# Numerators of eight token tiles per product, all value tiles by way of DRAM, and a query stage in a written-out order

## The chip, the cores and the metric

One Trainium2 chip, one of its cores. A time is the device time of one launch in microseconds (us). The engines are named as in the profile: PE multiplies matrices (PEld is its weight load), DVE works on vectors, ACT evaluates activations and copies out of PSUM, POOL is the fourth engine with arithmetic of its own, SP issues the DMAs. Each engine works through its queue in order; semaphores carry the waits between them. The matmul results lie in PSUM, eight banks of 128 partitions by 512 float32, everything else in SBUF or in DRAM.

## The reference, cut to what matters

```python
# B, S, D, H = 1, 2048, 448, 16 ; Dh = 28
def _A_ref(x, wqkv, w_phi, wo):                      # linear attention
    q, k, v = split_heads(x @ wqkv)
    pq, pk  = einsum("bhsd,hdf->bhsf", q, w_phi), einsum("bhsd,hdf->bhsf", k, w_phi)
    phi_q   = concat([softmax(pq), softmax(-pq)], -1)   # 56 features a head
    phi_k   = concat([softmax(pk), softmax(-pk)], -1)
    kv, z   = einsum("bhsf,bhsd->bhfd", phi_k, v), phi_k.sum("s")
    num     = einsum("bhqf,bhfd->bhqd", phi_q, kv)
    den     = einsum("bhqf,bhf->bhq", phi_q, z)[..., None] + 1e-6
    return (num / den) merged over heads @ wo
def _B_ref(x, wqkv, wo):                             # softmax attention
    q, k, v = split_heads(x @ wqkv)
    return softmax(q @ k.T * Dh ** -0.5) @ v merged over heads @ wo
g = sigmoid((x * gate_w).sum(-1, keepdims=True))
out = g * _A_ref(A_x, ...) + (1 - g) * _B_ref(A_x, ...)
```

Both branches take `A_x`. All inputs and the output are float32.

## The kernel before, in words

The program has four stages. Numbers of tokens: 2048 make 16 tiles of 128.

1. **Projection** (0 to some 62 us). x is split into a high part `XH` and a low part `XL` (float32r each), both kept in SBUF for all 2048 tokens; the keys and queries of branch B are multiplied in blocks of 512 tokens (`proj_qk`) and written to DRAM (`qkd`).
2. **Key stage** (62 to 180 us). For each of the 16 token tiles the folded key weights give the key features of branch A (`tok_major`, `features1`, the exponential in `take_exps`, `features2`), `value_a` the values, and `kv_add` sums their product in PSUM.
3. **Query stage** (180 to 350 us), a loop over q from 0 to 26 with conditions on q. Its steps:
   - *query tile* (16 times): eleven matmuls `pq` against `wqA_s`; `features1` copies it out on ACT (L465), takes the largest and smallest value of a head on DVE (L467, L468), and subtracts them on POOL (L471, L473) into one of four buffers `feat`; then the exponential on ACT (L476); `features2` sums and inverts on DVE (L483, L484) and multiplies on POOL (L485); `turn` transposes on DVE (L548) into `fT`. `fT` holds four tiles and has one buffer, so tile 4 can be turned only when the numerators of tiles 0 to 3 are multiplied.
   - *value tile* (`value_b`): eleven matmuls `pvb` against `wvB_s`, copied out on ACT (L765). Ten of the 16 tiles (`EARLY`) go into a buffer `ve` and by DMA to DRAM (`v_d`), to be fetched later by `load_early`; the buffers `vb` in which they end lie in memory that is free only later. Tile 7 is written straight into `vb` late in this stage, tiles 11 to 15 after it.
   - *numerators* (`numer(n, half)`): for four token tiles, 32-row by 32-column weights from `KV` against 128 columns of `fT`, 64 calls a half. A call of float32 stands in the trace as two matmuls. The result `pn` takes both `mx` buffers of PSUM.
   - *normalisation* of the eight results of 128x1024 (four n, two i): `normalize1` copies to `oU` on ACT (L416) and fetches the denominators by DMA (L421), `normalize2` inverts them on DVE (L427, L428) and spreads them through DRAM by DMA (L432, L437), `normalize3` multiplies on DVE (L443), `normalize4` splits into `oT` on ACT, DVE and POOL (L451, L452).
   - *output of branch A* (`out_a(n, a)`, 16 times): twelve matmuls `poa` against `woA_s`, scaled on ACT into `ga` (L602, two buffers) and written to DRAM by DMA (L603).
   - *maximum units* (`mx_unit`): four matmuls of 28 rows by 512 columns, a Relu of 128x1024 on ACT (L305) and two reductions on DVE (L307), for the upper bound that the softmax of branch B subtracts. Of the 56 units two are called in the first two rounds of this stage and 20 are spread by `tick`, which counts matmuls and calls a unit at each count in `pace["at"]`; the first twelve of these fall into the last rounds of the query loop (Relu tile `rl_s`), the other eight lie between the matmuls of the value tiles 11 to 15 (Relu tile `rl`).
   - at q = 21 the first query and key stacks of branch B are fetched from DRAM into `qk0` (`load_q(0)`, `load_nm(0)`, `load_k(0, 0)`).
   After the loop the pool `ta` and the weights `wp` are closed. In the memory that comes free lie the second half of `vb`, four further key stacks `kst`, one query stack `qst`; POOL clears the stacks (L781) before the DMAs fill them (L786). The value tiles 11 to 15 are multiplied in this time.
4. **Attention** (350 us to the end). For each group of four heads, block of 512 queries and tile of 128 keys: scores `st` (L1030), exponential on ACT (L1033), products with `vb` (L1129), and between them the rest of the maxima (`pm`, L339) and the output `pob`.

The order on PE, DVE, ACT and POOL is that in which the program is written (`manual_schedule`); the order of the DMAs on SP is the scheduler's. A tile that takes the place of another waits until the other has been read for the last time. PSUM in the query stage has two buffers of one bank (`s`, for `pq`, `pvb`, `poa`), two of two banks (`mx`) and one of two banks (`md`).

Of the kernel before, what the change touches and what calls it, by code (L numbers as in the profile page):

```python
# [8 lines left out]
F32 = mybir.dt.float32  # L9
# [31 lines left out]
def gated_mix_kernel(ctx, tc, xT, wqkB, wvB, wvA, wkAT, wqAT, phi, woA, woB,  # L41
# [39 lines left out]
    EARLY = (0, 1, 2, 3, 4, 5, 6, 8, 9, 10)  # L81
# [18 lines left out]
    XH = front.tile([P, 4, S], F32R, name="XH")  # L100
    XL = front.tile([P, 3, S], F32R, name="XL")
# [19 lines left out]
    def x3(t):  # L121

        for b in range(4):
            yield b, XH[:, b, t], 0
            yield b, XH[:, b, t], 1
            if b < 3:
                yield b, XL[:, b, t], 0

# [247 lines left out]
    def split_x(t, raws):  # L376
        tt = slice(t * 512, (t + 1) * 512)
        for b, raw in zip((0, 2), raws):
            nc.scalar.copy(XH[:, b:b + 2, tt], raw)

            def low(b=b, raw=raw):
                if b == 0:
                    nc.vector.tensor_sub(XL[:, 0:2, tt], raw, f32(XH[:, 0:2, tt]))
                else:
                    (nc.gpsimd if t > 1 else nc.vector).tensor_sub(
                        XL[:, 2, tt], raw[:, 0, :], f32(XH[:, 2, tt]))
                    nc.vector.tensor_sub(XH[64:, 3, tt], raw[64:, 1, :], f32(XH[64:, 3, tt]))

            lows.append(low)
# [22 lines left out]
    def normalize1(pool, pn, nm, n):  # L412

        oU = pool.tile([P, n, 512], F32, tag="oU", name=f"oU{nm}", bufs=1 + n)
        if n == 2:
            nc.scalar.copy(oU, pn)  # L416
        else:
            nc.vector.tensor_copy(oU[:, 0, :], pn[0])
        den = pool.tile([P, n, 16], F32, tag="den", name=f"den{nm}", bufs=2)
        for i in range(n):  # L420
            nc.sync.dma_start(den[:, i, :], oU[DH:P:32, i, :])  # L421
        return oU, den

    def normalize2(pool, oU, den, nm, n, eps):

        if eps:
            nc.vector.tensor_add(den, den, eps_s.unsqueeze(1).to_broadcast([P, n, 16]))  # L427
# [3 lines left out]
        for k in range(n):  # L431
            nc.sync.dma_start(rd[:, k * 512:(k + 1) * 512], den[:, k, :])  # L432
# [29 lines left out]
    def features1(pp, nm, eng):  # L462
# [3 lines left out]
        ext = bd.tile([P, 2, H], F32, tag="ext", name=f"ext{nm}", bufs=3)  # L466
# [77 lines left out]
    def turn(u):  # L544

        if u % 4 == 0:
            fT_of[u // 4] = ta.tile([P, 4, 2 * H, 32], F32, tag="fT", name=f"fT{u // 4}", bufs=1)
        nc.vector.transpose(fT_of[u // 4][:, u % 4].rearrange("p h t -> p (h t)"),  # L548
                            fq.pop(u).rearrange("p h f -> p (h f)"))

    def numer(n, half):

        if half == 0:
            num[n] = [ps_mx(f"pn{n}_{i}", False) for i in range(2)] if n else pn_next
        pn = num[n]
        for g in (2 * half, 2 * half + 1):
            for b in range(2):
                for a in range(4):
                    for c in range(4):
                        rows, k = slice(32 * a, 32 * a + DH), 2 * g + b  # L560
                        nc.tensor.matmul(pn[a // 2][32 * c:32 * c + 32, a % 2, g * P:(g + 1) * P],  # L561
                                         KV[rows, k // 4, k % 4 * P + 32 * c:k % 4 * P + 32 * c + 32],
                                         fT_of[n][rows, :, 2 * (4 * g + c) + b, :],
                                         start=b == 0, stop=b == 1, tile_position=(32 * a, 32 * c),
                                         skip_group_check=True)
        for i in range(2 * half):
            num[n, i] = normalize1(ta, pn[i], f"a{n}_{i}", 2)
# [27 lines left out]

    def out_a(n, a):
        po = ps_s(f"poa{n}_{a}")
        run(po[:, :D], [x for g in range(NG)
                        for x in out_passes(oTs[n, a // 2][a % 2], g * P, woA_s[:, :, :, :D], g)],
# [60 lines left out]
    def first_units():  # L660
# [12 lines left out]
        for b in range(4):  # L673
            w, x = wB[0][:, :, b, :], XH[:, b, :512]
# [3 lines left out]
            if b < 3:  # L678
                nc.vector.tensor_sub(XL[:, b, :512], raw[b][:, 1, :], f32(x))
                todo = [(0, x), (1, x), (0, XL[:, b, :512])]  # L680
# [63 lines left out]
    def value_tile(i):  # L744
# [3 lines left out]
        nc.gpsimd.memset(v[:, :, :, 28:32], 0.0)  # L748
        nc.gpsimd.memset(v[:, :, :, 28:29], 1.0)
        return v  # L750

    def value_b(t, mid=None):
        pv = ps_s(f"pvb{t}")
        tok_major(pv, t, wvB_s, D, mid)
        if t in EARLY:
            k = EARLY.index(t)
            if k % 2 == 0:
                ve = ta.tile([P, 2, 512], F32, tag="oT", name=f"ve{k}", bufs=4)
# [86 lines left out]
    VALUE = {2: 0, 3: 1, 4: 2, 5: 3, 6: 4, 7: 5, 8: 6, 9: 8, 10: 9, 17: 10, 22: 7}  # L845

    def norm2(q, early):
        for i in range(2):
            if q % 4 == 3 and 7 <= q <= NT + 3 and early == (q > 16):
                n = (q - 6) // 4  # L850
                num[n, i] = normalize2(ta, *num[n, i], f"a{n}_{i}", 2, True)

    def norm4(q, at):
        n, i = (q - 10) // 4, q % 4 - 2
        if 10 <= q <= NT + 7 and i >= 0 and at == "BB"[i]:
            oTs[n, i] = normalize4(ta, num.pop((n, i)), f"a{n}_{i}", 2)

    for q in range(NT + 11):
        n4 = (q - 6) // 4
        take_acts()  # L860
        if q < 2:
            take_exps()
        if q == 0:
            wvB_s = weights(2, "wvB_s")
            woA_s = weights(3, "woA_s")
            load_split(wvB_s, "wvB")
            load_split(woA_s, "woA")
        if q in (0, 2):
            kv_add(NT - 4 + q)
            kv_add(NT - 3 + q)  # L870
        if q == 2:
# [5 lines left out]
        if q == 4:  # L877
# [4 lines left out]
        if q == 21:  # L882
            w = f32(weights(1, "qk0"))
            for b in range(4):
# [475 lines left out]
```

## Time and profile before

| what | value |
|---|---|
| time, median of 3 runs | 1016.03 us (1015.34 to 1017.53) |
| the profiled execution | 1018.57 us, span 1016.8 us |
| PE busy | 1000.4 us, 98% of the span |
| ACT, DVE, POOL busy | 794.4, 674.6, 232.6 us |
| mean granted clock of PE | 0.989 |
| DMA, mean over the span | 110 GB/s |

The span runs from the first to the last instruction of the profiled execution; the run's own time holds 1.8 us more. A matmul's recorded duration is its latency, and neighbours overlap, so what one costs is read from the chain of work or from the distance of starts, not from its mean duration. Rows of windows give the busy time of each engine in a stretch, with the number of instructions in brackets, then the granted clock, the share of the DMA engines and what they moved. "Idle before" is time in which an engine waited, with what ended it.

### The profile page before, as it was taken

What the parts mean: (1) busy time and instruction counts of PE and PEld (TensorE: products, weight loads), DVE (VectorE), ACT (ScalarE), POOL (GpSimd) and SP (SyncE); (2) the same over time, 40 slices, a digit from 0 to 9 for tenths busy, and PEclk for the clock granted to TensorE, in tenths of its full rate; (3) what the DMA queues carried; (4) which work ended last, traced back from release to release, by engine and by line L of the source; (5) the groups of instructions that cost most, each with busy time, mean ns of one, the idle gap of its engine ahead of it and who ended that gap; (6) DMA issues with size and microseconds to landing.
All of it is one profiled execution on the core that took longest, in us unless ns stands there. A gap on an engine that the chain in (4) does not pass through costs nothing.

```text
span 1016.8 us, 19271 instructions
## 1 busy us (share of the span) xinstructions
PE 1000.4 (98%) x7116; PEld 560.0 (55%) x7116; DVE 674.6 (66%) x1351; ACT 794.4 (78%) x1491; POOL 232.6 (23%) x227
## 2 busy tenths in 40 slices
PE   9999999999997999999999999999999999999998
PEld 8877777888875633333333333333333444454656
DVE  6567776768744678888788888888886544534202
ACT  5456655544434799999999999999999999979682
POOL 1265445668611510310102101002011011001010
PEclk9999999999888999999999999999999999999999
DMA  8975221613257572223434223343242364306141
GB/s 303 319 242 181 88 85 34 206 45 87 84 141 201 138 162 58 61 59 91 103 82 99 69 67 98 84 109 83 56 89 69 83 138 90 105 33 150 56 109 55
DMA packets 74232, 112.10 MB, mean 110 GB/s; under 512 B 21561, under 2 KB 33513, under 8 KB 73993
## 3 DMA queue, kind: packets, MB, share of 16 engines
q1 hardware_dynamic: 74138, 110.87, 40.1%
q8 instruction: 56, 0.92, 0.4%
q14 instruction: 38, 0.31, 0.1%
HBM read 76.31 MB, written 34.10 MB: 109 GB/s over the span
## 4 chain that ended last, share of the span: by engine, by line
PE 95%; DMA 2%; DVE 1%; issue 1%; ACT 0%; SPq 0%; POOL 0%; POOLq 0%; DVEq 0%; ACTq 0%
PE st L1030 28%; PE pv L1129 24%; PE pm L339 9%; PE pqk L118 6%; PE pk L137 4%; PE pva L137 4%; PE poa L118 3%; PE pq L118 3%; PE pob L118 3%; PE pmb L298 2%; PE pn L561 2%; PE pvb L118 2%; PE pvb L137 1%; PE pqk L689 1%; DMA qk<-qkd 1%; PE pkv L503 1%
## 5 line engine op out<-in xcount | busy, mean ns | idle before, releaser
L1033 ACT ACTIVATE p<-st 128x512 f32<-128x512 f32 x1020 | 527.7, 642 | 26.0 <-PE st L1030 26.0
L350 DVE TENSOR_REDUCE part<-pm 128x1 f32<-128x512 f32 x450 | 287.3, 684 | 150.8 <-PE pm L339 150.8
L1129 PE MATMUL pv<-p,vb 128*32 128x512 f32 x2048 | 263.7, 602 | 0.0
L343 ACT ACTIVATE rl<-pm 128x512 f32<-128x512 f32 x200 | 124.7, 623 | 14.2 <-PE pm L339 13.2
L339 PEld LDWEIGHTS pm<-kc,qc 28*128 28x128 f32 x800 | 38.3, 181 | 167.6 <-issue 101.4
L443 POOL TENSOR_TENSOR oUb<-oUb,rsb 128x512 f32<-128x512 f32 x15 | 19.3, 1287 | 458.2 <-DMA rsb<-rdb 180.2
L1030 PE MATMUL st<-qk,kst 128*128 128x512 f32 x384 | 116.2, 425 | 0.0
L1030 PE MATMUL st<-qst,kst 128*128 128x512 f32 x384 | 114.8, 423 | 0.0
L347 DVE CUSTOM_DVE_ANT_0 rl<-pm,rl 128x512 f32<-128x512 f32 x150 | 102.0, 680 | 0.0
L339 PE MATMUL pm<-kc,qc 28*128 28x512 f32 x800 | 101.4, 495 | 0.0
L1129 PEld LDWEIGHTS pv<-p,vb 128*32 128x32 f32 x2048 | 47.4, 108 | 95.5 <-issue 89.0
L1030 PEld LDWEIGHTS st<-qst,kst 128*128 128x128 f32 x384 | 64.3, 187 | 38.1 <-ACT p L1033 16.5
L1030 PEld LDWEIGHTS st<-qk,kst 128*128 128x128 f32 x384 | 63.8, 187 | 38.1 <-ACT p L1033 18.1
L307 DVE CUSTOM_DVE_ANT_0 rl<-pmb,rl 128x512 f32<-128x512 f32 x88 | 56.4, 679 | 27.0 <-ACT rl L305 27.0
L305 ACT ACTIVATE rl<-pmd 128x1024 f32<-128x1024 f32 x44 | 45.2, 1028 | 28.4 <-PE pmd L298 19.8
L118 PE MATMUL pqk<-XH,wB 128*128 128x512 f32 x192 | 59.8, 398 | 0.0
L118 PE MATMUL poa<-woA_s,oTa 128*128 128x448 f32 x192 | 47.9, 400 | 0.0
L626 ACT CAST ev<-pqk 128x512 fp32r<-128x512 f32 x28 | 16.1, 588 | 36.7 <-PE pqk L118 30.3
L118 PEld LDWEIGHTS poa<-woA_s,oTa 128*128 128x128 f32 x192 | 38.9, 208 | 6.5 <-issue 3.2
L476 ACT ACTIVATE feat<-feat 128x896 f32<-128x896 f32 x32 | 30.6, 956 | 12.6 <-POOL feat L473 12.6
L118 PEld LDWEIGHTS pqk<-XH,wB 128*128 128x128 f32 x192 | 35.2, 188 | 9.1 <-issue 2.2
L1144 DVE SCALAR_TENSOR_TENSOR acc<-pob,gate,acc 128x448 f32<-128x448 f32 x12 | 8.2, 684 | 47.3 <-PE pob L118 47.3
(172 smaller groups left out, 1359.5 us busy)
## 6 DMA issues: line engine op xcount, KB each, us to landing
qkd<-ev SPq DMA_DIRECT2D x28, 512.0 KB
qk<-qkd SPq DMA_DIRECT2D x48, 224.0 KB
kst<-qkd SPq DMA_DIRECT2D x48, 224.0 KB
qst<-qkd SPq DMA_DIRECT2D x32, 224.0 KB
od<-oTb SPq DMA_DIRECT2D x48, 112.0 KB
rsa<-rda SPq DMA_DIRECT2D x32, 128.0 KB
rsb<-rdb SPq DMA_DIRECT2D x15, 256.0 KB
kc<-qkd SPq DMA_DIRECT2D x64, 56.0 KB
```

The source lines that it names most:

```text
L118: nc.tensor.matmul(dst, l, r, start=i == 0, stop=i == len(todo) - 1, skip_group_check=mid is not None)
L137: nc.tensor.matmul(dst[:, :n], l, r, start=i == 0, stop=i == len(todo) - 1, skip_group_check=True)
L305: nc.scalar.activation(rl, pd, AF.Relu)
L307: nc.vector.tensor_tensor_reduce(rl[:, i, :], pb[:, i, :], rl[:, i, :], 1.0, LOWEST, ALU.add, ALU.max, part[:, col + i:col + i + 1])
L339: nc.tensor.matmul(pm[j], mxs[("qc", gq)][js, qt * P:(qt + 1) * P], mxs[("kc", g, kb)][js, :], start=True, stop=True, tile_position=(32 * ...
L343: nc.scalar.activation(rl, pm[kb], AF.Relu if kb < 3 else AF.Copy)
L347: nc.vector.tensor_tensor_reduce(r, pm[j], r, 1.0, LOWEST, ALU.add, ALU.max, part[:, col + j:col + j + 1])
L350: nc.vector.tensor_reduce(part[:, col + j:col + j + 1], pm[j], AX.X, ALU.max)
L476: exps.append(lambda: nc.scalar.activation(fx, fx, AF.Exp))
L1030: nc.tensor.matmul(st, kst_of[(gq // NQ, kt // 4)][:, j, (kt % 4) * P:(kt % 4 + 1) * P], qst_of[gq][:, j, :], start=True, stop=True)
L1033: nc.scalar.activation(p, st, AF.Exp, scale=SCALE)
L1129: nc.tensor.matmul(pv[32 * j:32 * j + 32, :], vb[kt // 8][:, kt % 8, 4 * g + j, :], pt[j], start=kt == 0, stop=kt == NT - 1, tile_position ...
```

## The change

- `numer(k)` takes eight token tiles and half the head groups at a time: `fT` holds eight tiles (twice the memory, still one buffer), a matmul has 256 columns instead of 128, and there are 4 x 64 calls instead of 8 x 64. Tiles 8 to 15 can be turned only when both halves of the first eight are multiplied.
- x is split into tiles of 1024 tokens. Once the query and value tiles 0 to 7 are done, the places of the first half hold the results `oU` and their high parts `hi` (`place`). `lo` takes the tag `oT`, shared with the buffers `ve`, now three of them.
- The denominators of a result go in one DMA instead of two, both to `den` and to `rd`.
- All 16 value tiles go by way of DRAM within the query stage; each half of `vb` is fetched with one `load_early` of eight tiles. The five value tiles and eight units that stood behind the query loop are now inside it.
- The loop over q is replaced by a list of steps, in whose order PE, DVE, ACT and POOL work. Letters: p query, f `features2`, t `turn`, v value, e exponentials, n numerators, r m c the parts of the normalisation (inverse, multiplication, split), o output, u unit, k `kv_add`, j `proj_qk`, z the first stacks, y `load_early(0)`, w start of the 20 paced units, l the Relu tiles in the place of `fT`.

```diff
-    EARLY = (0, 1, 2, 3, 4, 5, 6, 8, 9, 10)
+    EARLY = (0, 1, 2, 3, 4, 5, 6, 7, 8, 9, 10, 11, 12, 13, 14, 15)
...
-    XH = front.tile([P, 4, S], F32R, name="XH")
-    XL = front.tile([P, 3, S], F32R, name="XL")
+    X = [[[front.tile([P, 2 - low * b, 1024], F32R, tag=f"x{2 * low + b}" if t == 0 else f"y{2 * low + b}",
+                      name=f"{'XL' if low else 'XH'}{t}_{b}") for b in range(2)] for t in range(2)]
+         for low in range(2)]
...
-        den = pool.tile([P, n, 16], F32, tag="den", name=f"den{nm}", bufs=2)
-        for i in range(n):
-            nc.sync.dma_start(den[:, i, :], oU[DH:P:32, i, :])
+        den = pool.tile([P, 16 * n], F32, tag="den", name=f"den{nm}", bufs=1 + n)
+        nc.sync.dma_start(den, oU[DH:P:32].rearrange("p n q -> p (n q)"))
...
-        for k in range(n):
-            nc.sync.dma_start(rd[:, k * 512:(k + 1) * 512], den[:, k, :])
+        nc.sync.dma_start(rd, den)
...
+    def numer(k):
+
+        n, half = divmod(k, 2)
+        pn = pn_next if k == 0 else [ps_mx(f"pn{k}_{i}", False) for i in range(2)]
+        for g in range(2):
             for b in range(2):
                 for a in range(4):
                     for c in range(4):
-                        rows, k = slice(32 * a, 32 * a + DH), 2 * g + b
-                        nc.tensor.matmul(pn[a // 2][32 * c:32 * c + 32, a % 2, g * P:(g + 1) * P],
...
+                        rows, z = slice(32 * a, 32 * a + DH), 4 * half + 2 * g + b
+                        nc.tensor.matmul(pn[a // 2][32 * c:32 * c + 32, a % 2, g * 256:(g + 1) * 256],
...
+                                         fT_of[n][rows, :, 8 * (2 * half + g) + 2 * c + b, :],
...
+    def place(nm, n, half, i, ty):
+
+        if half == 0:
+            j = {"oU": (0, 1, 1, 2), "hi": (2, 0, 0, 1)}[nm][2 * n + i]
+            places[nm, n, i] = front.tile([P, 2, 2, 512], ty, tag=f"x{j}", name=f"{nm}{n}_{i}")
+        return places[nm, n, i][:, half]
+
+    def part_of(k):
+
+        n, half, i = k // 4, k // 2 % 2, k % 2
+        o, hi = num.pop(k), place("hi", n, half, i, F32R)
+        if i == half == 0:
+            lo = front.tile([P, 2, 512], F32R, tag="x3", name=f"lo{k}")
+        else:
+            lo = ta.tile([P, 2, 512], F32R, tag="oT", name=f"lo{k}", bufs=3)
+        for j in range(2):
+            nc.scalar.copy(hi[:, j], o[:, j])
+            (nc.gpsimd if j else nc.vector).tensor_sub(lo[:, j], o[:, j], f32(hi[:, j]))
+        oTs[k] = hi, lo
...
+    def units_open():
+        pace.update(n=0, at=[77, 92, 101, 104, 110, 115, 121, 127, 133, 139, 148, 155, 164, 169, 176, 181, 188, 195, 202, 209])
...
+    for w in (
+            "j6", "k12", "f-1", "u", "p0", "p1", "s", "s", "j7", "e", "f0", "u", "E", "g", "e", "k14",
+            "K", "p2", "f1", "v0", "e", "p3", "f2", "t0", "t1", "v1", "x", "e", "S", "p4", "f3", "t2",
+            "v2", "e", "p5", "f4", "t3", "v3", "e", "p6", "f5", "t4", "v4", "e", "p7", "p8", "f6", "t5",
+            "v5", "e", "f7", "t6", "v6", "e", "p9", "t7", "f8", "v7", "e", "p10", "n0", "e", "v8", "n1",
+            "r0", "f9", "r1", "t8", "p11", "f10", "p12", "v9", "r2", "r3", "t9", "e", "f11", "t10", "f12", "v11",
+            "e", "m0", "p15", "p13", "v10", "c0", "t11", "v12", "m2", "e", "p14", "t12", "c2", "f13", "v13", "e",
+            "f14", "f15", "t13", "e", "w", "o0.0", "t14", "m1", "o0.1", "t15", "m3", "c1", "o1.0", "c3", "o1.1", "B",
+            "n2", "o0.2", "n3", "l", "r4", "o0.3", "r6", "r5", "r7", "m4", "o1.3", "c4", "o1.2", "m6", "v14", "c6",
+            "m5", "o2.0", "c5", "z", "m7", "v15", "o3.0", "c7", "y", "o2.1", "o3.1", "o3.2", "o2.3", "o2.2", "o3.3",
+    ):
...
-    for t in range(11, NT):
...
-            value_b(t, tick)
...
+    load_k(0, 1)
+    load_early(1, 8)
+    while mxs["u"] < NF - 2:
+        mx_unit()
+    for i in range(2):
+        scores(0, i)
+        if mxs["u"] < NF:
+            mx_unit()
```

More of the change, by code (lines that the diff above doesn't have):

```diff
@@ L747, in value_tile @@
         v = pool.tile([P, NT // 2, H, 32], F32, name=f"vb{i}")
[L748 to L749 removed]
+        n = sum(t // 8 == i for t in EARLY)
+        if n < 8:
+            nc.gpsimd.memset(v[:, n:, :, 28:32], 0.0)
+            nc.gpsimd.memset(v[:, n:, :, 28:29], 1.0)
         return v
@@ L858, in gated_mix_kernel, with query @@
[L858 to L871, printed above, removed]
+    def query(q):
+        pq = ps_s(f"pq{q}")
+        tok_major(pq, q, wqA_s, D)
+        fq[q] = features1(pq, f"q{q}", nc.gpsimd)
@@ L947, in gated_mix_kernel @@
-        n = (q - 9) // 4
-        if 9 <= q <= NT + 6 and q % 4 < 3:
-            i = q % 4 - 1
-            if i in (0, 1):
-                num[n, i] = normalize3(*num[n, i], 2)
+        elif w == "x":
+            kv_out(kvT)
+        else:
+            do[w[0]](*[int(x) for x in w[1:].split(".") if x])
     rls.clear()
```

185 lines of the change are left out of this document (77 added, 108 removed).

## The prediction, made before the changed kernel was run

> **What bounds the kernel now.** I read the page's head first, then the windows, the waits of PE, the chain of work.
>
> ```profile
> span 1016.8 us, 19271 instructions
> PE 1000.4 (98%) x7116; PEld 560.0 (55%) x7116; DVE 674.6 (66%) x1351; ACT 794.4 (78%) x1491; POOL 232.6 (23%) x227
> ```
> ```profile
> 179.80:350.40 170.60, 159.66 (x1758) 130.84 (x1755) 114.54 (x212) 83.65 (x117) 89.33 (x84) 0.94 0.44 125
> ...
> 304.00:324.00 20.00, 13.27 (x55) 9.52 (x54) 8.99 (x20) 8.75 (x12) 2.59 (x3) 0.88 0.91 230
> 354.00:378.00 24.00, 24.00 (x152) 8.94 (x151) 18.68 (x37) 23.38 (x48) 3.91 (x4) 1.00 0.73 163
> ```
> ```profile
> 266.00:268.00 2.00, 2.00 (x12) 1.60 (x6) 0.00 (x0) 1.93 (x2) 1.38 (x1) 0.50 0.00 0
> ```
> ```profile
> PE pmd L298 <- ACT rl_s L305: 6.7, 2, 4.3
> PE pn L561 <- issue: 3.8, 2, 2.4
> ```
>
> PE is the bound, also in the query stage: 159.7 of its 170.6 us, and no other engine is above 115. PE is idle there for 10.9 us, nearly all of it in the two waits, and the granted clock is 0.94, so about 0.06 x 170.6 = 10.2 us more go to half clock. The two belong together: the chain below has an idle piece of 1.41 us at 262.70, and the window from 266 to 268 shows the clock at 0.50. With four such stops (two on `pmd`, two on `pn`) a stop costs its length and about 2.6 us. The longest, 4.3 us, comes from SP: the write of `ga` stood behind the fetches of the first stacks, so ACT had no `ga` to write.
>
> ```profile
> 182.25 0.43 PE pmb L298 x2
> ...
> 190.90 0.92 PE pkv L503 x64
> ...
> 210.74 2.23 PE pq L118 x11
> 212.97 1.84 PE pn L561 x102
> ...
> 243.92 2.44 PE poa L118 x12
> ...
> 262.70 1.41 issue
> ...
> 302.63 3.72 DMA rsa<-rda
> ...
> 316.01 4.57 DMA gad<-ga
> ```
>
> So a query tile costs PE 2.23 us, and a value tile, also of eleven matmuls, as much; an output 2.44; a unit 0.43, which I raise to 0.63, since a switch between shapes costs some 0.2; half a numerator, 128 matmuls of which the chain holds 102, 1.84.
>
> **The numerators.** Eight halves of 1.84 make 14.7 us. Afterwards there are four products of 128 matmuls with 256 columns. Here 128 columns take 14.3 ns a matmul; `pkv`, with 56 columns, takes 0.92 us / 64 = 14.4. The same distance for 56 and 128 columns speaks for a limit by issue, not by columns. The price of 256 columns isn't in the trace: it lies between 1.84 us a product (issue alone) and 3.7 (by columns). I take 2.0, near the row. Saved: 14.7 - 8.0 = 6.7 us, with ends 0 and 7.3.
>
> **What is free.** The split of x adds no instruction. The denominators lose 16 DMAs of some 0.55 us on SP, off PE's path. Six more value tiles go to DRAM and back, 1.5 MB each way; their products are moved, not added. The old stops go with the order that made them: -10.9 idle and -10.2 half clock. What is late next follows.
>
> **The first new wait: DVE before the outputs.** The rows are groups of 212 to 262 us, in which POOL works too, then the instructions on `oUa` over the stage (ns, least, median, most; a multiplication and a split are longest beside POOL).
>
> ```profile
> L548 DVE STREAM_TRANSPOSE fT<-feat 128x1024 f32<-128x1024 f32 x9 | 10.5, 1188 | 0.0
> L483 DVE TENSOR_REDUCE fsumq<-feat 128x32 f32<-128x896 f32 x8 | 8.6, 1075 | 0.0
> ...
> L468 DVE TENSOR_REDUCE extq<-pcq 128x16 f32<-128x448 f32 x9 | 5.5, 607 | 0.0
> L467 DVE TENSOR_REDUCE extq<-pcq 128x16 f32<-128x448 f32 x9 | 5.4, 604 | 9.8 <-ACT pcq L465 9.8
> ...
> L484 DVE RECIPROCAL fsumq<-fsumq 128x32 f32<-128x32 f32 x8 | 2.8, 353 | 0.3
> ```
> ```profile
> L485 POOL TENSOR_TENSOR feat<-feat,fsumq 128x896 f32<-128x896 f32 x9 | 16.3, 1812 | 0.7
> L471 POOL TENSOR_TENSOR feat<-pcq,extq 128x448 f32<-128x448 f32 x9 | 8.5, 944 | 13.4 <-DVE extq L467 13.4
> ```
> ```profile
> L421 SPq DMA_DIRECT2D dena<-oUa x16: 522/540/649, 220.0 to 292.3; - x16
> L451 ACT CAST oTa<-oUa x16: 613/618/632, 237.1 to 313.0; 128x512 fp32r<-128x512 f32 x16
> L416 ACT COPY oUa<-pn x8: 1012/1017/1018, 219.0 to 290.3; 128x1024 f32<-128x1024 f32 x8
> L443 DVE TENSOR_TENSOR oUa<-oUa,rsa x8: 1219/1636/1902, 235.2 to 310.9; 128x1024 f32<-128x1024 f32 x8
> L452 DVE TENSOR_TENSOR oTa<-oUa,oTa x8: 692/907/1130, 238.0 to 313.1; 128x512 fp32r<-128x512 f32 x8
> ```
>
> Starts lie some 0.08 us closer than durations, so: transpose 1.14, sum and inverse 1.39, the two extremes 1.07, a multiplication 1.8, a split 1.04 and, from 0.19 (at 292.96, below) and an inverse as long as L484, a denominator 0.46. Up to `n0` nothing is late: a query tile needs 3.6 us of DVE and about as much of POOL (two subtractions, one multiplication), and query and value tile give 4.46 on PE. Behind `n0` the list holds for DVE, up to `c2` on which `o0.0` waits: four sums 5.6, five transposes 5.7, five extremes 5.4, four denominators 1.8, two multiplications 3.6, two splits 2.1, together 24.2. It can begin only when the first denominators have landed, 3.0 us behind `n0` (copy 1.0, issue 0.55, landing 1.35 as below), and loses about 1 waiting for ACT's copies. That is 28.2; PE has five query tiles, six value tiles and `n1`, 26.6. New stop: 1.6 us. From `c2` to the last transpose, on which `n2` waits, DVE needs 9.4, PE's four outputs 9.8 and the half clock, so nothing waits there.
>
> **The second: the outputs of the later eight tiles.** `o2.0` needs both left results of `n2` and `n3`.
>
> ```profile
> 290.43 2.36 SPq L421 DMA_DIRECT2D dena<-oUa  x4
> ...
> 304.64 2.04 SPq L786 DMA_DIRECT2D qk<-qkd  x4
> ...
> 312.57 3.33 SPq L786 DMA_DIRECT2D qk<-qkd  x4
> ...
> 339.66 1.88 SPq L786 DMA_DIRECT2D kst<-qkd  x4
> ```
> ```profile
> 292.96 0.19 DVE L427 TENSOR_TENSOR dena<-dena,eps_s 128x32 f32<-128x32 f32 x1 [0.41 <-DMA dena<-oUa]
> ```
> ```profile
> L307 DVE CUSTOM_DVE_ANT_0 rl_s<-pmb,rl_s 128x512 f32<-128x512 f32 x24 | 15.6, 688 | 16.4 <-ACT rl_s L305 16.4
> ```
> ```profile
> L305 ACT ACTIVATE rl_s<-pmd 128x1024 f32<-128x1024 f32 x12 | 12.3, 1025 | 5.9 <-PE pmd L298 5.3 <-ACT ga L602 0.5
> ```
>
> The first two denominators were issued by 291.61 and there at 292.96: landing 1.35. From the end of `n3`, PE has three outputs, a value tile and four units, 12.1 us. `hi` of `c4` takes the place that `o1.2` reads last, so ACT can write it only 8.6 us on. In DVE's order follow: cast 0.57, split 0.62 (POOL is idle now), a unit's two reductions with their reads 1.5, the multiplication of `m6` 1.25, two units 3.1, split 0.62, end 16.3. The DMA chain of `m6` (copy 1.0, denominators 1.9, inverse 0.5, to DRAM another 1.9, back 5.1 by three issues as at 339.66 and the 3.72 of the chain's row, 0.6 for SP's other issues) is done at 11.0, before DVE asks. Stop: 4.2 us. The bounds are 0 (splits finish in a gap between units) and 8.
>
> **The third: SP.** The first stacks now stand at `z`, and the writes of `o3.0` and of value tile 15 behind them. Their fetches held SP from 304.64 to 315.9, 11.3 us; `ga` of `o3.1` waits for 1 + 11.3 + 0.6 + 4.57 = 17.5 us behind `o2.0`, when PE is done with value tile, three outputs and seven units after 14.0 and can work some 1.6 longer. Stop: 2 us, with ends 0 (the scheduler issues them earlier) and 4.3 as before.
>
> **The fourth: the start of attention.** Five value tiles and eight units covered the clearing and filling of the stacks. Now nothing lies between the last output, whose end I call E, and the scores.
>
> ```profile
> 337.19 7.13 POOL L781 MEMSET kst<- 128x2048 f32 x4
> 344.26 1.81 POOL L781 MEMSET qst<- 128x2048 f32 x1
> ```
> ```profile
> 350.44 0.86 PE L1030 MATMUL st<-qk 128*128 128x512 f32 x3
> ...
> 358.18 1.14 PE L1030 MATMUL st<-qk,kst 128*128 128x512 f32 x4
> ...
> 371.88 1.07 PE L1129 MATMUL pv<-p,vb 128*32 128x512 f32 x8
> ```
>
> Clearing can begin when the last unit has left the place of `fT`, by its Relu 1.0 and its reductions 1.5 at about E + 2.8 (1.9 to 3.7). The first stack is clear at E + 4.6, issued by E + 7.0, there by E + 9.5; it is needed 7.7 us behind the first scores, which begin 1.2 behind E: a stop of 0.6. The second eight value tiles, 2 MB, are issued behind all five clearings, at E + 11.7, and needed at 371.88 - 350.44 + 1.2 = E + 22.6. From E + 5.1 the queue has them, two to three stacks of 0.9 MB and some 1 MB of key rows, 4.3 to 5.7 MB; at 230 GB/s (the row of 304) they end at E + 24 to E + 30. I take a stop of 4.4. With one half clock: 0.6 + 4.4 + 2.6 = 7.6 us.
>
> **The sum.** -6.7 (numerators) - 10.9 - 10.2 (old stops) + 1.6 + 4.2 + 2.0 (new ones) + 7.8 (their half clock) + 7.6 (attention) = -4.6 us. The profiled execution took 1018.57 us with a span of 1016.8, so 1014.0; the median of the runs is 2.5 lower, 1016.03, which gives **1011.4**.
>
> [...]
>
> **The rivals.**
> - *Attention's start is hidden anyway.* The fetch of 2 MB lands in time, as a long transfer goes first or faster than 230. The windows of 304 show DMA engines at 0.91 with only 230, which speaks against it; that the stacks are needed one at a time speaks for it. Without the 7.6: 1003.8.
> - *256 columns cost twice 128.* The same 14.4 ns for 56 columns speaks against it. Then 6.7 comes back: 1018.1. [...]
> - *Slower: the second half of the values comes late.* At the 163 GB/s of 354 to 378 the 5.7 MB need 35 us and end at E + 40, a stop of 17.4 in place of 5.0: 1011.4 + 12.4 = 1023.8. It decides from E + 29 on, where the forecast's gain of 4.6 is gone. For it speaks that this row is the very place; against it, that DMA is busy there at 0.73 only.
> [...]
>
> **How the numbers follow.** Forecast 0.45 (its own range 1004 to 1017, from the ends of its stops), hidden start 0.20, twice the columns 0.10, late values 0.20, short stops free 0.05. A measurement tells 0.2%, 2 us, from no change. Faster: 0.40 of the forecast, hidden start, short stops, 0.02 of the columns: 0.67. Slower: late values, 0.05 of the others: 0.25. The rest, 0.08, is no change. The range of 1001 to 1024 reaches from the hidden start with numerators at 1.84 and a shorter second stop to the late values; about 0.2 lies outside.
>
> **What the profile after would show.** 512 matmuls `pn` at 14 to 17 ns distance (29: columns). PE idle before `poa` on DVE's or ACT's split, some 2 and 4 us; `pmd` waiting for ACT behind `gad`; half clock behind each. A first wait of `st` for `kst` below 2 us, and of `pv` for `vb` some 4. If the query stage shows no stops, or `pv` waits over 10 us, the forecast is wrong.

## The result, and the profile after

The changed kernel takes 1011.09 us (median of five runs, 1009.93 to 1012.40) against 1016.03 for the kernel before in the same comparison (1015.32 to 1017.53): a ratio of 0.9949, 95% interval 0.9935 to 0.9964. The forecast of 1011.4 us hit the time. It did not hit all of the reasons. The profiled executions show a larger difference than the medians, 1018.57 to 1010.6, or 8.0 us of span, because that of before was a long one and that of after a short one.

The page's head of the changed kernel, then its windows (179.67 to 333.50 is the query stage up to the first scores) and the waits of PE from 175 to 360 us (line, what it waited for: total us, times, longest us):

```profile
span 1008.8 us, 18258 instructions
PE 990.9 (98%) x6604; PEld 549.4 (54%) x6604; DVE 674.2 (67%) x1351; ACT 794.6 (79%) x1491; POOL 233.4 (23%) x229
```
```profile
179.67:333.50 153.83, 146.69 (x1303) 118.78 (x1303) 113.50 (x210) 81.87 (x117) 81.67 (x80) 1.00 0.46 144
361.00:381.00 20.00, 17.99 (x102) 7.13 (x103) 13.22 (x30) 15.77 (x32) 3.79 (x3) 0.91 0.46 114
366.00:370.00 4.00, 4.00 (x27) 1.39 (x19) 2.30 (x8) 2.90 (x6) 0.25 (x1) 0.68 0.60 160
```
```profile
PE pmb L305 <- DVE part L314: 4.0, 5, 1.1
PE poa L125 <- DVE lo L592: 1.6, 2, 1.3
...
```

Both waits that headed the list of before are gone, `pmd` for the Relu (6.7 us) and `pn <- issue`; of `pmd` 0.4 us are left. Two waits of ACT in before, from 295 to 335 us, show that the two `pmd` stops had different causes: the Relu of the longer one (4.3 us) stood behind `ga`, that of the other (2.4 us) behind a split that waited for DVE's multiplication.

```profile
ACT ga L602 <- DMA gad<-ga: 5.8, 1, 5.8
...
ACT oTa L451 <- DVE oUa L443: 3.5, 1, 3.5
```

What replaced these waits is of the same order, 153.83 - 146.69 = 7.1 us of idle time after 10.9 before, but in more and shorter pieces, and the granted clock reads 1.00 over the whole stage, where it was 0.94. The only half clock of this execution runs from 365.11 to 368.53 us, in the attention stage. Two more traces of the same kernel (`c_after` and `c2_after`, below) have half clock in the query stage as well: both read 0.96 from 262 to 300 us, about 0.04 x 38.0 / 0.5 = 3 us of it.

The timelines of PE (start, length, the matmuls, in brackets the idle time before them and its releaser), first of after, then of before:

```profile
231.22 2.76 PE L565 MATMUL pn<-fT,KV 28*32 28x256 f32 x128
265.08 0.47 PE L125 MATMUL poa<-woA_s,lo 128*128 128x448 f32 x1 [1.29 <-DVE lo L592]
...
335.88 0.96 PE L1048 MATMUL st<-qk 128*128 128x512 f32 x3 [1.53 <-ACT p L1007]
343.79 0.83 PE L346 MATMUL pm<-kc,qc 28*128 28x512 f32 x4 [0.76 <-POOL kc L214]
356.50 1.17 PE L1048 MATMUL st<-qk,kst 128*128 128x512 f32 x4 [0.88 <-DVE part L357]
363.01 0.70 PE L346 MATMUL pm<-kc,qc 28*128 28x512 f32 x4 [2.02 <-POOL kc L214]
381.00 1.16 PE L1048 MATMUL st<-qst,qk 128*128 128x512 f32 x4
```
```profile
260.43 2.27 PE L561 MATMUL pn<-fT,KV 28*32 28x128 f32 x154
264.10 2.19 PE L561 MATMUL pn<-fT,KV 28*32 28x128 f32 x102 [1.41 <-issue]
283.03 3.06 PE L561 MATMUL pn<-fT,KV 28*32 28x128 f32 x212
288.45 1.36 PE L561 MATMUL pn<-fT,KV 28*32 28x128 f32 x44 [2.36 <-issue]
389.16 1.14 PE L1030 MATMUL st<-qst,qk 128*128 128x512 f32 x4
```

Two marks split the gain. The third score product, freed of its own wait, would stand at 335.88 - 1.53 = 334.35; before it stood at 350.44. So the way to the end of the query stage is 16.1 us shorter. The second query block starts at 381.00 instead of 389.16, so 46.65 us after the first mark instead of 38.72: the start of attention gave 7.9 back. The rest of the program is equal: 16.1 - 7.9 = 8.2, and the spans differ by 8.0.

The chain of waits of after, at the start of attention, shows where the 2.02 comes from:

```profile
336.15 4.44 POOL kst L816 x3
...
342.41 7.93 DMA vb<-vd
...
350.71 9.27 DMA kst<-qkd
...
359.99 1.71 DMA kc<-qkd
...
361.71 1.26 POOL kc L214
```

POOL clears the stacks, only then are the second eight value tiles fetched (2 MB in 7.93 us), behind them the key stack, behind that the keys whose difference `kc` the maxima need.

### The profile page after: what moved, and what is told of

The parts are those of the page before. It is cut to its first block, busy times and chain, and to the rows that moved or that the text cites. A ratio compares the mean times of both kernels' runs of the same rounds, so it can differ in the third digit from the quotient of the medians.

```text
span 1008.8 us, 18258 instructions
## 1 busy us (share of the span) xinstructions
PE 990.9 (98%) x6604; PEld 549.4 (54%) x6604; DVE 674.2 (67%) x1351; ACT 794.6 (79%) x1491; POOL 233.4 (23%) x229
## 4 chain that ended last, share of the span: by engine, by line
PE 89%; DVE 4%; DMA 3%; POOL 2%; issue 1%; ACT 1%; SPq 0%; DVEq 0%; POOLq 0%; ACTq 0%
PE st L1048 27%; PE pv L1143 24%; PE pm L346 8%; PE pqk L125 6%; PE pk L144 4%; PE pva L144 4%; PE pq L125 3%; PE pob L125 3%; PE pvb L144 2%; PE pmb L305 2%; PE poa L125 2%; PE pqk L722 1%; DMA kst<-qkd 1%; DMA vb<-vd 1%; PE pn L565 1%
## 5 line engine op out<-in xcount | busy, mean ns | idle before, releaser
L1048 PEld LDWEIGHTS st<-qst,kst 128*128 128x128 f32 x384 | 64.3, 187 | 38.1 <-ACT p L1051 16.6
L314 DVE CUSTOM_DVE_ANT_0 rl<-pmb,rl 128x512 f32<-128x512 f32 x72 | 46.0, 677 | 23.6 <-ACT rl L312 23.6
L312 ACT ACTIVATE rl<-pmd 128x1024 f32<-128x1024 f32 x36 | 37.0, 1027 | 25.5 <-PE pmd L305 16.5
L658 ACT CAST ev<-pqk 128x512 fp32r<-128x512 f32 x28 | 16.1, 587 | 36.2 <-PE pqk L125 30.0
L1048 PE MATMUL st<-qk 128*128 128x512 f32 x124 | 37.7, 423 | 2.0 <-ACT p L1007 1.5
L125 PE MATMUL poa<-woA_s,hi 128*128 128x448 f32 x128 | 38.7, 377 | 0.3 <-ACT pcq L470 0.3
L144 PE MATMUL pk<-wkA_s,XH 128*128 128x448 f32 x128 | 38.9, 380 | 0.0
```

The costliest lines, as they stand in the source:

```text
L125: nc.tensor.matmul(dst, l, r, start=i == 0, stop=i == len(todo) - 1, skip_group_check=mid is not None)
L144: nc.tensor.matmul(dst[:, :n], l, r, start=i == 0, stop=i == len(todo) - 1, skip_group_check=True)
L312: nc.scalar.activation(rl, pd, AF.Relu)
L314: nc.vector.tensor_tensor_reduce(rl[:, i, :], pb[:, i, :], rl[:, i, :], 1.0, LOWEST, ALU.add, ALU.max, part[:, col + i:col + i + 1])
L1048: nc.tensor.matmul(st, kst_of[(gq // NQ, kt // 4)][:, j, (kt % 4) * P:(kt % 4 + 1) * P], qst_of[gq][:, j, :], start=True, stop=True)
```

## The experiments

Theory when they began: the numerators cost what the columns make of them, the old stops came from the old order, and the start of attention loses what it lost because no PE work covers clearing and fetching. The kernel before took 1017.75 us beside the first four, 1016.86 beside the next four, 1017.39 beside the last.

**Numerators of 128 columns in the new order** (`e1_n128`). The split of the token tiles is undone, all else stays:

```diff
-        for g in range(2):
+        for g, u in ((g, u) for g in range(2) for u in range(2)):
...
-    pn[a // 2][..., g * 256:(g + 1) * 256], ..., fT_of[n][rows, :, ...]
+    pn[a // 2][..., g * 256 + u * P:g * 256 + u * P + P], ..., fT_of[n][rows, 4 * u:4 * u + 4, ...]
```

> The changed kernel, but each numerator product of 256 columns is made as two of 128 (the order stays the new one). In the changed kernel's trace a product of 128 matmuls with 256 columns takes 2.69 us, before one with 128 columns took 1.84, so two would take 3.68. Theory 1, PE is the bound in the query stage and the numerators lie on its path: 4 x (3.68 - 2.69) = 4.0 us slower than the changed kernel, about 1015. Theory 2, DVE sets the pace around the numerators (PE already waits there for DVE), so PE's saving is hidden: within 1 us of the changed kernel, about 1011 to 1012.

It took 1021.15 us, 1.0035 of before (1.0022 to 1.0049), so both theories missed. Its waits, and its windows from stop to stop:

```profile
PE pn L565 <- issue: 5.8, 3, 2.1
PE pvb L144 <- issue: 0.9, 1, 0.9
```
```profile
235.20:242.90 7.70, 5.82 (x256) 4.68 (x256) 2.24 (x6) 2.92 (x4) 1.70 (x1) 1.00 0.25 71
242.90:284.40 41.50, 37.73 (x384) 33.62 (x383) 34.52 (x42) 17.35 (x28) 28.63 (x24) 0.96 0.35 106
284.40:293.90 9.50, 7.76 (x256) 6.27 (x256) 0.55 (x2) 2.56 (x3) 0.00 (x0) 0.82 0.18 47
```

The stops that I had put down to the old order are here in the new one, and more of them. Between them lie 256, 384 and 256 matmuls with as many weight loads (one record of 384 is missing), so 512, 768 and 512 PE instructions: each a multiple of 256. The two stops of before have the same distance:

```profile
263.40:287.50 24.10, 21.99 (x384) 19.25 (x384) 13.94 (x19) 8.37 (x13) 10.90 (x8) 0.86 0.33 96
```

This is 263.40 to 287.50, from the one stop to the other: again 384 + 384 = 768. Nothing that the profile's waits show is waited for. That points to the supply of PE's instructions in blocks of 256. The pages of before and of the changed kernel list a DMA queue of kind `instruction` (packets, MB, share of the DMA engines), first before, then changed:

```profile
q8 instruction: 56, 0.92, 0.4%
```
```profile
q8 instruction: 52, 0.85, 0.4%
```

These are packets of 16 KiB (0.92 MB / 56 and 0.85 MB / 52), about one for every 256 of PE's matmuls and loads (14232 in before, 13208 in the changed kernel). At the two stops of before such a packet lands at 262.88 and at 286.96 us, 1.22 and 1.49 us before the stop ends, and the next one starts at 265.23 and at 289.49, 1.13 and 1.04 us after it. In `e1_n128` the windows around two of the stops, 279 to 286 and 289 to 296 us, hold two such packets each. A stop costs 0.9 to 2.4 us here.

The common condition would be a long run of these small matmuls: with its load each is two instructions in 14.3 ns, so 256 instructions last 1.83 us. This is the third theory: supply. In before the two numerator halves of the last two products follow each other directly, 256 matmuls in a row; those of the first two have a value tile between them, and no stop.

**The loops over `a` and `c` exchanged** (`e2_swap`), so that neighbouring matmuls share other rows of weights.

```diff
-                for a in range(4):
-                    for c in range(4):
+                for c in range(4):
+                    for a in range(4):
```

> The changed kernel with the two inner loops of the numerators exchanged: successive matmuls go to another row group instead of another column group of the same rows. If the 21.0 ns between matmuls of 256 columns (14.3 with 128, 14.4 with 56) come from neighbours that read the same 32 rows, the distance falls to 14 to 17 ns, a product to 1.9 to 2.2 us, and the time by 2 to 3 us, to about 1008. If they come from the columns themselves, or from the issue, the product stays at 2.69 us and the time at 1011.

1009.89 us, 0.9922 of before (0.9904 to 0.9940), which is not apart from the changed kernel itself on another occasion (0.9928 below). The product kept its length:

```profile
230.73 2.76 PE L565 MATMUL pn<-fT,KV 28*32 28x256 f32 x128
```

So the 2.69 us from start to start (21.0 ns a matmul) do not come from the order of the tiles.

**Four value tiles and the scores behind the query loop again** (`e3_late4`).

```diff
-    EARLY = (0, 1, 2, 3, 4, 5, 6, 7, 8, 9, 10, 11, 12, 13, 14, 15)
+    EARLY = (0, 1, 2, 3, 4, 5, 6, 7, 8, 9, 10, 11)
...
-    load_early(1, 8)
+    load_early(1, 4)
+    for t in range(12, NT):
+        value_b(t, (lambda i: scores(0, i // 3 - 1) if i in (4, 7) else None) if t == NT - 1 else tick)
```

> The changed kernel with the value tiles 12 to 15 behind the query loop again (the others by way of DRAM, as changed), the first scores between the matmuls of the last one. Theory 1: the start of attention loses less, since the four tiles cover the clearing and the fetches (the changed kernel loses some 6.6 us there: waits of 1.5, 0.8, 0.9 and 2.0 and a half clock); but the four tiles filled PE while DVE worked, so without them DVE's stretch before the first output and the stretch behind the last numerator stop PE for up to 8.9 us, partly at half clock: 3 to 8 us slower than the changed kernel in all. Rival: the tiles gave no cover inside, then 4 to 6 us faster, about 1006.

1012.59 us, 0.9954 (0.9937 to 0.9971). Waits and the window of the start of attention:

```profile
PE poa L125 <- ACT hi L591: 6.9, 3, 4.0
PE poa L125 <- DVE lo L592: 2.0, 1, 2.0
...
```
```profile
336.00:375.00 39.00, 39.00 (x232) 19.52 (x232) 25.15 (x58) 33.62 (x63) 15.67 (x13) 1.00 0.68 166
```

With PE work over the clearing, the start of attention has no idle time at all: the second query block stands 38.71 us behind the mark, as in before (38.72). But the outputs now wait for splits by 8.9 us, since the value tiles that gave ACT and DVE their time are gone from between them. The value tiles cover one place or the other. The edit also halves the second fetch of values, to 1 MB, so cover and the smaller fetch are not told apart.

**The kernel before with its first stacks fetched later** (`e4_latez`).

```diff
-        if q == 21:
+        if q == 24:
```

> The kernel before, with one condition changed: the first stacks are fetched at q = 24 instead of q = 21. Theory: the stop of 4.3 us (and about 1.6 at half clock) came from the write of ga behind these fetches on SP, so it goes or shrinks, and the time falls by 3 to 6 us, to 1010 to 1013. Rival: SP's order is not that of the program, the fetches stand at the same place and the time stays at 1016; or the stop only moves to the next ga, or the stacks come late for the first scores, and the time stays or rises.

1017.73 us, 0.9990 (0.9977 to 1.0003): no gain. Waits, and one window; the profiled execution is the shortest of the twelve, 1012.64 us:

```profile
PE pmd L298 <- ACT rl L305: 4.2, 1, 4.2
PE pn L561 <- issue: 3.4, 2, 2.3
...
```
```profile
262.00:300.00 38.00, 34.60 (x618) 28.73 (x612) 25.12 (x41) 18.58 (x27) 16.51 (x13) 1.00 0.40 107
```

The stop on `ga` only moved to the value tiles, as the rival had it. The window is the side finding: with the same two `issue` stops this execution kept full clock where that of before had 0.82. Half clock came behind the stops of 1.41 and 2.36 us of before, and not behind those of 1.15 and 2.26 us here.

The traces show a grid behind this. In before half clock starts at 264.49, 288.38, 308.86 and 322.52 us, so 7, 6 and 4 times 3.413 us apart, and it lasts 6.83, 6.83, 3.41 and 3.41 us, one or two such units. In the changed kernel's trace it starts at 365.11 us and, behind the last instruction, at 1010.23, 189 units on. Counted from the first instruction the grid lies elsewhere in each of the two: 365.11 is 29.5 units from 264.49. In `e4_latez` the half clock behind the stop of 4.2 us ends between 332.19 us, where two matmuls `pvb` take 0.91 us, and 332.94, where one takes 0.37; that puts a border near 332.7, and the two rows of `e4_latez` below stand 15 and 14 units ahead of it. The rows are units around the second `issue` stop, two of before (the second row holds two units), then two of `e4_latez`:

```profile
284.97:288.38 3.41, 1.12 (x79) 0.83 (x65) 1.92 (x2) 1.52 (x3) 0.31 (x1) 1.00 0.66 190
288.38:295.21 6.83, 6.76 (x58) 5.28 (x58) 3.24 (x6) 3.17 (x6) 1.76 (x3) 0.50 0.20 55
```
```profile
281.52:284.93 3.41, 2.35 (x178) 2.04 (x158) 0.67 (x1) 0.00 (x0) 0.00 (x0) 1.00 1.01 247
284.93:288.34 3.41, 2.21 (x51) 1.83 (x52) 2.59 (x3) 2.82 (x5) 1.60 (x2) 1.00 0.40 124
```

In before 2.29 us of the stop fall into one unit (3.41 - 1.12), and half clock follows for two; in `e4_latez` the border, where those 14 units put it, cuts a stop of 2.26 us into 1.06 and 1.20, and none follows.

**The kernel before with a value tile between the halves of every product** (`e5_sep`), the direct test of supply.

```diff
-    VALUE = {2: 0, 3: 1, 4: 2, 5: 3, 6: 4, 7: 5, 8: 6, 9: 8, 10: 9, 17: 10, 22: 7}
+    VALUE = {2: 0, 3: 1, 4: 2, 5: 3, 6: 4, 7: 5, 8: 6, 10: 8, 14: 9, 18: 10, 22: 7}
```

> The kernel before, with its value tiles at other rounds only: round 10 multiplies value tile 8, round 14 tile 9, round 18 tile 10, so that each pair of numerator halves now has a value tile between its two halves; round 9 and round 17 have none. Theory A (PE runs out of instructions where more than some 200 matmuls of 14.3 ns stand in a row): the two waits 'pn <- issue', 2.36 and 1.41 us, are gone, 3.8 us, and with them the half clock of 262 to 300 us, some 5 us; the other two stops stay, so 1008 to 1012 us. Theory B (the stops belong to the place in the program, or to who writes the operands): the waits stay or move, 1015 to 1018 us. Theory C (round 9 without a value tile leaves DVE behind): a new wait of PE for a transpose of up to 1 us, and no more than that.

```profile
PE pmd L298 <- ACT rl_s L305: 6.3, 2, 3.6
PE pn L561 <- DVE fT L548: 4.8, 2, 2.7
...
```

No `issue` wait is left, as supply says, though the same 1024 matmuls run at the same 14.3 ns. The time is 1018.78 us, 1.0018 of before (1.0004 to 1.0033), where theory A had 1008 to 1012: the rounds that lost their value tile now wait 4.8 us for the transposes, more than the 3.8 that went and the 1 that I had allowed, and half clock follows three of the four stops. The gain in mechanism became a loss in order.

**The first scores ahead of the last output** (`e6_scores`): two score products and their exponentials as a step before `o3.3`.

```diff
-            ... "o2.3", "o2.2", "o3.3",
+            ... "o2.3", "o2.2", "h", "o3.3",
```

> The changed kernel, with the first two score products and their exponentials put before the last output of branch A instead of behind the closing of the stage. Theory A (at the start of attention PE loses by short waits in a row, the first of them 1.5 us for the exponentials of the first scores): that wait goes and 1 to 2 us are gained on the changed kernel, so 1009 to 1010 us where the changed kernel gives 1011. Theory B (the start is bound by the chain of clearing, fetch of the values, fetch of the keys and key differences): the wait of 2.0 us for the key difference grows by what was gained, and the time stays within 0.5 us of the changed kernel.

1012.81 us, 0.9950 (0.9932 to 0.9967), on a chip where the changed kernel itself (`c_after`) gave 1010.26, 0.9928 (0.9908 to 0.9947). The wait of 1.5 us went, and the exponentials now stand on ACT ahead of the last Relu, whose first reduction (of two) ends when the clearing starts. The chain of waits, then POOL's timeline, of this kernel and of the changed one:

```profile
338.73 0.69 DVE rl_s L314
```
```profile
339.42 7.03 POOL L816 MEMSET kst<- 128x2048 f32 x4 [8.69 <-PE poa L125]
```
```profile
333.55 7.04 POOL L816 MEMSET kst<- 128x2048 f32 x4 [4.64 <-PE poa L125]
```

The clearing begins at 339.42, where it began at 333.55 in the changed kernel, and PE waits 3.9 us for `kc`, instead of 2.8. POOL's idle time is put down to the last output (`poa`); that it was the reduction is read from the equal times, 338.73 + 0.69.

**The second half of the values fetched first** (`e7_vbfirst`), **the difference, one stack, then the values** (`e9_mix`), **the difference alone** (`e10_diffs`). Three orders of POOL's work at the start of attention:

```text
 e7_vbfirst:  load_early(1, 8)   ahead of the four stacks
 e10_diffs:   take_diffs(0)      ahead of the four stacks
 e9_mix:      take_diffs(0); kst.append(stack("kst1", True)); load_early(1, 8)   then three stacks
```

> The changed kernel, with the fetch of the second eight value tiles issued ahead of the clearing of the key stacks instead of behind it. Theory B (chain of clearing, values, keys, key difference): the fetch starts some 8 us earlier, the wait of 2.0 us for the key difference at 361 goes, and with it 1.6 us of half clock: 2 to 3.5 us faster than the changed kernel, 1007.5 to 1009 us. Rival: the stacks' fetches now queue behind 2 MB, and the scores wait for the second key stack some 2 to 4 us instead: same time or up to 3 us slower.

> The changed kernel, with the clearing of the key stacks reordered on POOL: first the key difference that the maxima wait for, then the first stack, then the fetch of the second eight value tiles, then the other stacks. In the seventh run the fetch ahead of all clearing took away the wait of 2.0 us at 361 but had the key difference wait 3.6 us. Theory B (POOL's order at the start of attention is what costs): both waits for the key difference go, 2.0 and 0.8 us with some 1.6 us of half clock, and the time is 2 to 4 us below the changed kernel. Rival: the rest of the stacks is cleared later and the scores wait for them by as much: within 1 us of the changed kernel.

> The changed kernel, with only the key difference taken before the clearing of the stacks. Theory B: the first wait for it, 0.8 us, goes, and the later chain (clearing, values, keys) moves back by its 1.3 us: 0 to 0.8 us faster than the changed kernel, less than can be told. Rival: the wait of 2.0 us at 361 grows by 1.3, and the time is up to 1.5 us longer.

They took 1013.28, 1013.78 and 1012.52 us: 0.9961 (0.9945 to 0.9976), 0.9972 (0.9959 to 0.9985) and 0.9952 (0.9937 to 0.9968), where the changed kernel on the same chip gave 0.9928 for the first and 0.9941 (0.9927 to 0.9955, 1010.94 us, `c2_after`) for the other two. Each took away the wait it aimed at and got another. The waits of PE that are new or larger, of the three kernels in that order:

```profile
PE pm L346 <- POOL kc L214: 3.6, 1, 3.6
```
```profile
PE st L1048 <- DMA kst<-qkd: 5.7, 1, 5.7
```
```profile
PE pm L346 <- POOL kc L214: 2.1, 1, 2.1
PE st L1048 <- DVE part L354: 1.7, 1, 1.7
```

With the values first, POOL stood still for their place until 336.9 and came to the difference 3.4 us later. In the mix there is no wait for the difference, but the stack's fetch shares the DMA with 2 MB of values and lands late:

```profile
340.58 9.74 DMA kst<-qkd
```

The rival of `e9_mix` held, with a loss of 2.8 us where it allowed 1: from the mark to the second query block it needs 47.98 us, `e7_vbfirst` 47.87, `e10_diffs` 48.70, the changed kernel 46.65 (46.65 and 46.48 in its two repeats). Clearing, values, stacks and keys pass through one POOL and one set of DMAs, and the order only chooses who waits.

**128 columns with something between all runs** (`e8_split`): `e1_n128`, each product cut in two, other steps between.

```diff
-  "p10", "n0", "e", "v8", "n1", "r0", "f9", "r1", "t8", "p11", "f10", "p12", "v9",
+  "p10", "n0.0", "e", "v8", "n0.1", "r0", "f9", "r1", "p11", "n1.0", "f10", "v9", "n1.1", "t8", "p12",
...
-  "o1.1", "B", "n2", "o0.2", "n3", "l", "r4", "o0.3",
+  "B", "n2.0", "o1.1", "n2.1", "o0.2", "n3.0", "o0.3", "n3.1", "l", "r4",
```

> The kernel of the first experiment (new order, 128 columns a matmul, 256 matmuls a product), with each product cut into two runs of 128 matmuls and a query tile, a value tile or an output of branch A between all runs. Theory A (the stops of 5.8 us came where more than some 200 matmuls of 14.3 ns stand in a row): no wait 'pn <- issue' is left, the granted clock of 262 to 300 us is above 0.95, and the time is the changed kernel's plus 4 us for the numerators and up to 2 for the order, 1014 to 1017 us instead of 1021. Theory B (128 columns as such bring the stops, or the place in the program): some 6 us of these waits stay, 1019 to 1022 us.

Its waits of PE from 175 to 375 us hold no `issue`; two that do stand there, and two windows:

```profile
PE pmb L305 <- DVE part L314: 3.9, 3, 2.2
...
PE poa L125 <- ACT pcq L470: 2.6, 1, 2.6
```
```profile
262.00:280.00 18.00, 14.36 (x175) 11.77 (x174) 15.46 (x18) 8.48 (x14) 14.90 (x14) 0.81 0.42 119
300.00:320.00 20.00, 16.81 (x64) 10.35 (x63) 18.49 (x38) 12.64 (x18) 4.79 (x5) 0.74 0.60 173
```

The 6.7 us of `issue` waits are gone, all four. That is the second time, in another order, so it is the long runs of small matmuls, and not 128 columns as such, that bring them. The time is 1020.53 us all the same, 1.0040 (1.0025 to 1.0056): two other stops of 2.6 and 2.2 us (the second, for `part`, at 302 us), each with half clock behind it. Theory A had 1014 to 1017 and a clock above 0.95 from 262 to 300 us, where it reads 0.91; it left out what the moved steps do to DVE and ACT.

The changed kernel itself, on the two chips:

> The changed kernel itself, on the same chip as the other three, to have differences of 0.2% without the differences between chips: 1010 to 1013 us, 0.5% below the kernel before.

> The changed kernel itself once more, beside these three on their chip: 0.5 to 0.7% below the kernel before.

No version beat it by what can be told.

## Why the prediction was right, point by point

- **The numerators: mis-sized.** Saved were 14.7 - 4 x 2.69 = 4.0 us, not 6.7; "I take 2.0, near the row" was the failed step. The real price is almost in the middle of the two ends. 56 and 128 columns at one price (14.4 and 14.3 ns) said only that columns do not count up to 128. Beside the 4.0 us the change removed a cause of stops.
- **"The old stops go with the order that made them": right in the sum, wrong in the cause for two of the four.** The two `pmd` stops, one behind `ga` and one behind DVE, went with the order. The `pn` stops went because the products of 256 columns need half as many matmuls: the changed kernel has 128 in a row and then a value tile or an output, and with 128 columns in the same order, 256 in a row, they come back (`e1_n128`). Whether 256 matmuls of 21.0 ns in a row would stop is not tested. So the product of eight tiles is worth more than its 4.0 us, but by how much is not separated: `e1_n128` is some 10 us behind the changed kernel, of which 4.0 are the dearer products, 6.7 the stops, and some more half clock, less what DVE catches up meanwhile. The half clock of 10.2 was put somewhat too high. The rows do lose 10.2 us, nearly all of it while PE is busy, but not all work slows by that much: behind the two `issue` stops PE took 22.0 us for 384 matmuls and 17.2 for 112 in before, where `e4_latez` at full clock took 19.0 and 14.3, so 5.9 more where the rows lose 6.8. At that ratio, an estimate, 10.2 become 8.8.
- **First stop, 1.6 us before `o0.0`: right.** 0.27 for ACT and 1.29 for `lo`, at the place forecast.
- **Second, 4.2 before `o2.0`, and third, 2.0 for SP: right size, wrong shape.** DVE is behind there, but PE meets it in pieces, at the units (`pmb <- DVE part`, 0.5 to 1.1 us each) and 0.33 at the split, because each unit waits for the reductions of an earlier one. SP's stop didn't come: no output waits for `ga`. That is the lower end: the fetches of the first stacks stand behind the write of `o2.0` as forecast, but hold SP from 303.38 to 311.2, 7.8 us instead of 11.3. All idle time of the stage is 7.1 us, where the three made 7.8.
- **Their half clock, 7.8: wrong.** No wait of the stage is above 1.3 us, and in the profiled execution the clock stays at 1.00; even the 1.53 behind it has none. The two repeats read 0.96 from 262 to 300 us, so each loses some 0.04 x 38.0 = 1.5 us, and they have no wait above 1.3 us in the stage either. The step that failed is "a stop costs its length and about 2.6 us": 2.6 was the mean of two stops of before with 3.4 and two with 1.7, and a stop can also cost nothing. So the case to which I gave 0.05, short stops free, was nearly true for the query stage, but the time did not fall by that, since the other terms were dearer. Behind that stage half clock did come: the wait of 2.02 us brought 0.68 over 366 to 370 in the changed kernel.
- **The start of attention, 7.6: right size, other waits.** Measured 7.9: 1.53, 0.76, 0.88 and 2.02 idle make 5.2, and 0.09 x 20.0 = 1.8 us go to half clock from 361 to 381; 0.9 is spread. `pv` never waited for `vb`, so the 4.4 of the forecast isn't there; the late work is the key difference behind the values on the DMAs. That clearing and fetching without cover are the cause is borne out by `e3_late4`, where the start costs nothing, though there only half the values are left to fetch.
- **The sum.** By measured terms the query stage gives -4.0 (numerators) - 10.9 (idle before) - 8.8 (half clock) + 7.1 (idle after) = -16.6 where the marks show -16.1; the marks with 7.9 given back make -8.2, against a forecast of -4.6. The forecast of the profiled execution, 1014.0, was 3.4 too high; on the medians it came out right because the profiled execution of before lies 2.5 above its median and that of after 0.5 below. The hit is in part luck: 2.7 too much gain for the numerators against 6.3 to 7.8 too much loss for half clock, and a change forecast from an execution of before that was longer than its median.
- **The other rivals.** Late values did not come, the fetch went at 2 MB in 7.93 us and not at 163 GB/s. The hidden start did not come either. Twice the columns was half right.

## What to carry to other kernels

Where many small matmuls stand in a row, look for idle time that ends in `issue` and count the instructions between two such stops; fewer and larger matmuls (the changed kernel) or other work between runs of 128 (`e5_sep`, `e8_split`) took them away here, 3.8 us in before and 6.7 in `e1_n128`. Work that is moved out of a place has covered something there: name what it covered, since here half of the query stage's gain went back at the start of attention, and no reordering of that place alone regained it. A wait costs its length, and it may cost half clock as well: 3.41 or 6.83 us of it stood behind each of the four stops of before (1.41 to 4.30 us), none behind any wait of the changed kernel ahead of 361 us (0.25 to 1.53 us). In these two traces what it followed was the idle time within one unit of 3.41 us, though between 1.31 and 1.49 us that alone did not decide.

## What was not expected of the hardware

- PE stood still for 0.9 to 2.4 us at distances of 512 and 768 instructions, only where 256 matmuls of 14.3 ns stood in a row (154 to 256 of them done), never where 128 did. That it is the supply of instructions is my reading; it is borne out by the distances, by the two kernels in which breaking the runs took it away, and by the 16 KiB packets that land 1.22 and 1.49 us before the two stops of before end.
- A 32 x 32 tile costs 14.3 ns with 128 columns and 21.0 with 256, the latter in both orders of the tiles that were tried. Neither issue alone nor columns alone gives that; why stays open.
- Half clock does not follow from the length of the stop alone: 1.41 us had it in before, 1.15 and 2.26 in `e4_latez` had none, nor had 1.53 in the changed kernel. In before and in the changed kernel it starts whole units of 3.413 us apart. Cut into these units, the two traces show from 175 to 420 us: those at full clock with 1.31 (361.70, changed kernel), 1.41, 2.29, 2.43 and 3.18 us of idle time on PE (261.08, 284.97, 305.45 and 319.10, before) were followed by half clock; those with 1.12 (315.69, before), 1.20, 1.29 and 1.49 us (300.26, 262.71 and 334.39, changed kernel) were not, nor any with less. Between 1.31 and 1.49 both occur; what decides there stays open.
